# Load order, last output tile and stage shifts of a transformer block on one core

**Chip, cores, metric.** One Trainium2 chip (trn2), one of its cores. The metric is device time in microseconds (us) of one execution. A profile's span is 1.7 to 1.8 us shorter than the time of the same execution; where the text says "time" it means the former, where it says "span" the latter.

## The reference

Two sublayers over 2048 tokens of width 1024, in bfloat16, cut here to what matters:

```python
x = A_x                                            # (1, 2048, 1024)
h = x + A(layernorm(x), wq, wk, wv, wo, beta)      # 32 heads of 32, 4 segments of 512 tokens
#   per segment: p = softmax(causal q k^T), o = g * memory(q) + (1 - g) * (p v),  g = sigmoid(beta)
#   then the memory is updated with phi(k)^T v; after the 4th segment o @ wo
h2 = h + (silu(ln(h) @ w1) * (ln(h) @ w3)) @ w2    # inner width 3584
```

## The kernel before

The kernel writes no instruction order by hand. It builds a graph of operations, plans it with a list scheduler that has a cost for each operation, and then emits each engine's operations in the planned order. Each engine runs its queue strictly in that order. A table, `SHIFT`, moves each stage's priority a little; the table is the result of a search over plans. So any edit of the graph or of an assumed cost may reorder every engine.

Some words used below. A token tile is 128 tokens (`xs`). Its layer norm takes three steps: statistics, *apply* (subtract the mean, scale), and transposes on TensorE. PSUM is the memory that matmuls write to (`ps`); a result must be copied out before its bank is used again. A *score group* is the matmuls of q k^T for some heads; the *state matmuls* are those of phi(k)^T v that update the memory. A *dense* matmul here is one of 512 columns.

```python
SHIFT = {0: (113, 0), 1: (-194, 1), 2: (-667, 0), ...}     # stage: (rank shift, class shift)

    def dma(self, out, in_, cls=5, deps=(), eng="sp"):     # all loads and stores: one queue, SyncE
        ...
        o.bytes = n * SIZE[out.dtype]                      # the planner's landing time follows from this

    def constants(self):
        ...
        self.g.dma(self.beta[:, :], ..., cls=3)            # 8 KB, behind all the loads of class 0
        ...
        for n in range(4):                                 # "gcol": four small tanh on ScalarE
            self.act(self.gcol[r, :]..., bt, AF.Tanh, act_ns(8), cls=3, scale=0.5)

    def first_half(self):                                  # queries and keys of segment 0
        loads = [(self.xs[t][:, :], self.x2d[t * 128:(t + 1) * 128, :]) for t in range(4)]
        loads.insert(2, (wq[:, :, 0:256], sq[:, :, 0:256]))
        loads.insert(5, (wk[:, :, 0:256], sk[:, :, 0:256]))
        loads += [(wq[:, :, 256:512], ...), (wk[:, :, 256:512], ...), (wv[:, :, :], sv)]
        for out, in_ in loads:
            dma(out, in_, cls=0)
        for t in range(4):
            self.first_tile(t)         # statistics (VectorE for t = 0, 2; ScalarE for 1, 3), apply, transposes
        ...                            # then 16 projections by 128 columns of tokens

    def ffn_down(self, blk):
        ...
            cols = [(0, 512), (512, 256), (768, 256)] if t == 15 else [(0, 512), (512, 512)]
            for c0, n in cols:         # 28 matmuls, an add into ob, a store
```

The softmax here doesn't subtract the row's maximum and nothing guards it: scores larger than these inputs give would overflow.

## Time and profile before

| | before |
|---|---|
| time, first three runs | 896.26, 896.30, 896.68 us |
| span of the profiled run | 895.0 us |
| TensorE busy, as recorded (see the end of the experiments) | 880.6 us (98%) |
| TensorE idle in the first 20 us / after its last matmul | 4.0 us / 2.6 us |
| tile 1 ready on VectorE, applied | 7.76 us, 9.55 us |

Read it so: TensorE is the bound, so only what it waits for is worth anything. The largest single wait after the start is 1.23 us in the head. A late tile (2) blocks VectorE's queue, in which a ready tile (1) stands behind it. The lines themselves are in the prediction.

### The profile page before, as it was taken

What the parts mean: (1) busy time and instruction counts of PE and PEld (TensorE: products, weight loads), DVE (VectorE), ACT (ScalarE), POOL (GpSimd) and SP (SyncE); (2) the same over time, 40 slices, a digit from 0 to 9 for tenths busy, and PEclk for the clock granted to TensorE, in tenths of its full rate; (3) what the DMA queues carried; (4) which work ended last, traced back from release to release, by engine and by line L of the source; (5) the groups of instructions that cost most, each with busy time, mean ns of one, the idle gap of its engine ahead of it and who ended that gap; (6) DMA issues with size and microseconds to landing.
All of it is one profiled execution on the core that took longest, in us unless ns stands there. A gap on an engine that the chain in (4) does not pass through costs nothing.

```text
span 895.0 us, 13604 instructions
## 1 busy us (share of the span) xinstructions
PE 880.6 (98%) x5833; PEld 403.4 (45%) x5921; DVE 417.6 (47%) x631; ACT 287.9 (32%) x306; POOL 173.8 (19%) x226
## 2 busy tenths in 40 slices
PE   8999999999999999999999999999999999999998
PEld 5343444444444444444444444444444444444445
DVE  5784848585848485754555311211334333331111
ACT  6767766656565646111111100000111111110000
POOL 2553445353534343100200000000000000000000
PEclk9999999999999999999999999999999999999999
DMA  7899755634541221753475211113223221301110
GB/s 235 227 212 271 187 142 147 187 92 130 165 99 57 72 70 58 225 153 92 120 224 140 85 36 36 30 46 90 64 60 94 71 71 48 95 24 41 40 37 30
DMA packets 146540, 96.32 MB, mean 108 GB/s; under 512 B 45488, under 2 KB 133680, under 8 KB 146480
## 3 DMA queue, kind: packets, MB, share of 16 engines
q1 hardware_dynamic: 146480, 95.45, 38.8%
q8 instruction: 47, 0.77, 0.4%
q14 instruction: 13, 0.11, 0.0%
HBM read 76.55 MB, written 8.39 MB: 95 GB/s over the span
## 4 chain that ended last, share of the span: by engine, by line
PE 97%; issue 1%; DVE 1%; DMA 1%; ACT 0%; SPq 0%; ACTq 0%; DVEq 0%
PE ps L708 89%; PE ps L1107 4%; PE ps L1057 3%; DMA xs<-in_A_x_dram 1%; PE ps L985 0%; PE ps L1184 0%; ACT et L1069 0%; PE ps L1100 0%; DVE t L1260 0%; DVE hm L1265 0%; PE ps L720 0%; SPq L299 0%; DVE R L1163 0%; ACT sg L1257 0%; DVE Nsb L1171 0%
## 5 line engine op out<-in xcount | busy, mean ns | idle before, releaser
L708 PE MATMUL ps<-hnT,w1b 128*128 128x512 bf16 x876 | 218.4, 379 | 1.4 <-issue 0.3
L708 PE MATMUL ps<-hnT,w3b 128*128 128x512 bf16 x873 | 217.4, 379 | 1.5 <-issue 0.5
L1257 ACT ACTIVATE sg<-ps 128x512 bf16<-128x512 f32 x112 | 66.9, 597 | 403.1 <-PE ps L708 403.1
L708 PE MATMUL ps<-w2b,hm 128*128 128x512 bf16 (+1 forms) x907 | 195.3, 372 | 0.9
L1069 ACT ACTIVATE et<-ps 128x2048 bf16<-128x2048 f32 x80 | 150.0, 1875 | 39.3 <-PE ps L1057 38.9
L1260 DVE SCALAR_TENSOR_TENSOR t<-sg,ps 128x512 bf16<-128x512 bf16 x112 | 76.8, 685 | 169.4 <-ACT sg L1257 169.2
L708 PEld LDWEIGHTS ps<-w2b,hm 128*128 128x128 bf16 x924 | 90.4, 98 | 103.2
L708 PEld LDWEIGHTS ps<-hnT,w1b 128*128 128x128 bf16 x896 | 86.5, 98 | 105.5 <-issue 8.2
L708 PEld LDWEIGHTS ps<-hnT,w3b 128*128 128x128 bf16 x896 | 86.5, 98 | 105.4 <-issue 2.9
L1078 POOL TENSOR_SCALAR_AFFINE_SELECT et<-et 128x512 bf16<-128x512 bf16 x96 | 84.0, 881 | 126.2 <-ACT et L1069 126.0
L1265 DVE SCALAR_TENSOR_TENSOR hm<-t,ps 128x512 bf16<-128x512 bf16 x112 | 76.7, 686 | 50.5 <-PE ps L708 47.9
L1289 DVE TENSOR_TENSOR ob<-hr,ps 128x512 bf16<-128x512 bf16 (+1 forms) x33 | 22.1, 671 | 143.0 <-PE ps L708 143.0
L708 PE MATMUL ps<-wo,oT 128*128 128x512 bf16 x249 | 60.7, 380 | 0.6 <-issue 0.3
L708 PE MATMUL ps<-xnT,wp 128*128 128x512 bf16 (+1 forms) x345 | 59.7, 320 | 1.4 <-issue 0.6
L708 PE MATMUL ps<-hnT,wp 128*128 128x512 bf16 x250 | 59.0, 380 | 0.7 <-issue 0.6
L708 PEld LDWEIGHTS ps<-xnT,wp 128*128 128x128 bf16 x352 | 27.7, 98 | 26.9 <-issue 3.6
L708 PEld LDWEIGHTS ps<-wo,oT 128*128 128x128 bf16 x256 | 23.9, 98 | 29.8 <-issue 2.9
L708 PEld LDWEIGHTS ps<-hnT,wp 128*128 128x128 bf16 x256 | 23.6, 98 | 29.8 <-issue 3.8
L1200 POOL TENSOR_TENSOR oT<-Nsb,R 128x512 bf16<-128x512 f32 x23 | 35.8, 1569 | 4.1 <-DVE R L1197 4.1
L1163 DVE STREAM_TRANSPOSE R<-Rc 128x1024 f32<-128x1024 f32 x28 | 33.6, 1222 | 0.1
L1229 DVE TENSOR_TENSOR h<-h,ps 128x512 bf16<-128x512 bf16 x32 | 21.7, 680 | 25.1 <-PE ps L708 24.9
L1057 PE MATMUL ps<-qT,kT 32*128 32x128 bf16 (+3 forms) x512 | 31.7, 301 | 0.0
(82 smaller groups left out, 520.9 us busy)
## 6 DMA issues: line engine op xcount, KB each, us to landing
w1b<-in_B_w_dram SPq DMA_DIRECT2D x28, 512.0 KB, 3.9
w3b<-in_B_w_dram SPq DMA_DIRECT2D x28, 512.0 KB, 3.8
wp<-in_A_wv_dram SPq DMA_DIRECT2D x8, 1024.0 KB, 5.5
wp<-in_A_wq_dram SPq DMA_DIRECT2D x7, 1024.0 KB, 5.9
wp<-in_A_wk_dram SPq DMA_DIRECT2D x7, 1024.0 KB, 5.7
w2b<-in_B_w_dram SPq DMA_DIRECT2D x7, 1024.0 KB, 8.0
xs<-in_A_x_dram SPq DMA_DIRECT2D x16, 256.0 KB, 5.6
h<-in_A_x_dram SPq DMA_DIRECT2D x16, 256.0 KB, 3.7
```

The source lines that it names most:

```text
L708: return [e.matmul(p[0](gr), p[1], p[2], start=p[3], stop=p[4]) for p in part]
L1057: ins.append(e.matmul(self.bank(gr, j, 512 - 128 * kc, off), k[r, g0 + g, 128 * kc:128 * kc + 128], q[r, g0 + g, 128 * kc:512], start=True ...
L1069: return [e.activation(et[:, :, :], src, AF.Exp, scale=self.scale)]
L1078: self.pool_op(lambda e, v=v, pat=pat: e.affine_select(v, v, pattern=pat, compare_op=ALU.is_ge, fill=0.0, base=0, channel_multiplier=-1), ...
L1107: ins.append(e.matmul(self.ps[32 * i:32 * i + 32, b * 512 + 128 * kc:(b + 1) * 512], lhsT(i, kc, j), at[i, kc][:, j, :], start=kc == 0 and ...
L1163: return self.dve_op(lambda e: e.transpose(out, src), dve_ns(1024), [Rc[:, t, 2 * n:2 * n + 2, :]], [dst], 2)
L1200: self.either(lambda e, out=out, Ns=Ns, R1=R1: e.tensor_tensor(out, Ns, R1, op=ALU.add), 512, 2, [Ns, R1], [out], 2)
L1229: self.g.op("dve", dve_ns(512), lambda e, gr, hs=hs: [e.tensor_tensor(hs, hs, self.bank(gr), op=ALU.add)], reads=[hs], writes=[hs], cls=1, ...
L1257: self.g.op("act", act_ns(512), lambda e, gr, sg=sg: [e.activation(sg, self.bank(gr), AF.Tanh, scale=0.5)], writes=[sg], cls=0, group=gg)
L1260: e.scalar_tensor_tensor(t1, sg, 1.0, self.bank(gr), op0=ALU.add, op1=ALU.mult)], reads=[sg], writes=[t1], cls=0,
L1265: e.scalar_tensor_tensor(dst, t1, 0.5, self.bank(gr), op0=ALU.mult, op1=ALU.mult)], reads=[t1], writes=[dst], cls=0,
L1289: self.g.op("dve", dve_ns(n), lambda e, gr, hs=hs, ob=ob, n=n: [e.tensor_tensor(ob, hs, self.bank(gr, 0, n), op=ALU.add)], reads=[hs], wri ...
```

## The change

Its intent: load the third token tile before the first query weights, so that nothing blocks VectorE's queue; end the kernel on a smaller piece, so that less follows the last matmul; tell the planner how long the first loads really take, and search the table again for the new graph.

```diff
 SHIFT = {
-    0: (113, 0), 1: (-194, 1), 2: (-667, 0), ...
+    0: (-45, 0), 1: (-470, 0), 2: (43, 0), ...            # nearly every entry; cut here
-    def dma(self, out, in_, cls=5, deps=(), eng="sp"):
+    def dma(self, out, in_, cls=5, deps=(), scale=1.0):
-        o.bytes = n * SIZE[out.dtype]
+        o.bytes = n * SIZE[out.dtype] * scale
-        loads = [(self.xs[t][:, :], self.x2d[t * 128:(t + 1) * 128, :]) for t in range(4)]
-        loads.insert(2, (wq[:, :, 0:256], sq[:, :, 0:256]))
-        loads.insert(5, (wk[:, :, 0:256], sk[:, :, 0:256]))
-        loads += [...]
-        for out, in_ in loads:
-            dma(out, in_, cls=0)
+        x = [(self.xs[t][:, :], self.x2d[t * 128:(t + 1) * 128, :]) for t in range(4)]
+        loads = [x[0] + (1.04,), x[1] + (0.7,), x[2] + (1.2,),
+                 (wq[:, :, 0:256], sq[:, :, 0:256], 1.54), x[3] + (0.65,),
+                 (wk[:, :, 0:256], sk[:, :, 0:256], 0.74), ...]
+        for out, in_, scale in loads:
+            dma(out, in_, cls=0, scale=scale)
-            cols = [(0, 512), (512, 256), (768, 256)] if t == 15 else [(0, 512), (512, 512)]
+            cols = [(0, 512), (512, 256), (768, 128), (896, 128)] if t == 15 else [(0, 512), (512, 512)]
```

## The prediction

> **What bounds the kernel now.** I read the page first, then a table of stages, then the order of time at the two ends, then the list of waits. From the page, the busy line and the chain that ended last:
>
> ```profile
> PE 880.6 (98%) x5833; PEld 403.4 (45%) x5921; DVE 417.6 (47%) x631; ACT 287.9 (32%) x306; POOL 173.8 (19%) x226
> ...
> PE 97%; issue 1%; DVE 1%; DMA 1%; ACT 0%; SPq 0%; ACTq 0%; DVEq 0%
> ```
>
> TensorE is busy 98% of the span and makes up 97% of the chain; no other engine reaches half. So an edit counts only where it shortens TensorE's own stream or one of its few idle spells. The idle time is 895.0 - 880.6 = 14.4 us. The table of stages says where it lies (columns: window, its length, then busy time of PE, PEld, DVE, ACT, POOL, the granted clock, the DMA share and GB/s):
>
> ```profile
> 0.00:20.00 20.00, 16.00 (x181) 11.38 (x183) 9.70 (x28) 11.76 (x24) 5.06 (x22) 1.00 0.86 261
> ...
> 736.00:895.00 159.00, 155.62 (x738) 73.38 (x751) 38.21 (x57) 11.35 (x19) 0.00 (x0) 1.00 0.16 47
> ```
>
> The first 20 us hold 4.0 us of it, and the last stretch 3.4 us, of which 895.0 - 892.4 = 2.6 us follow the last matmul. The other 7 us are crumbs over 700 us. The granted clock is 1.00 everywhere, so no clock effect is to be had. The head, in order of time (start, length, engine, line, operation, tiles; in brackets the idle time before it and what ended it):
>
> ```profile
> 7.19 0.57 POOL L858 TENSOR_TENSOR rstd<-lnve,mhalf 128x1 f32<-128x1 f32 x1
> 7.70 0.90 PEld L708 LDWEIGHTS ps<-xnT,wp 128*128 128x128 bf16 x16 [0.74 <-DMA wp<-in_A_wq_dram]
> 7.70 1.07 PE L708 MATMUL ps<-xnT,wp 128*128 128x128 bf16 x16 [0.41 <-DMA wp<-in_A_wq_dram]
> 8.34 1.29 DVE L831 BATCH_NORM_STATS2 lnst<-xs 128x6 f32<-128x512 bf16 x2 [1.05 <-DMA xs<-in_A_x_dram]
> ...
> 9.55 0.72 DVE L862 TENSOR_SCALAR xs<-xs,lnst,rstd 128x512 bf16<-128x512 bf16 x2
> 10.00 0.55 PEld L720 LDWEIGHTS ps<-ident,xs 128*128 128x128 bf16 x8 [1.40 <-DVE xs L862]
> 10.00 0.72 PE L720 MATMUL ps<-ident,xs 128*128 128x128 bf16 x8 [1.23 <-DVE xs L862]
> ```
>
> This is the place the change aims at. Token tile 1's scale (rstd) is ready at 7.19 + 0.57 = 7.76 us, but VectorE applies it only at 9.55, because its in-order queue has the statistics of tile 2 ahead of it, and tile 2 lands at 8.34. TensorE, which has done its 16 matmuls for tile 0, sits idle 1.23 us until the apply. One load that comes late blocks a ready tile behind it. The tail:
>
> ```profile
> 887.20 0.69 DVE L1289 TENSOR_TENSOR ob<-hr,ps 128x512 bf16<-128x512 bf16 x1 [2.78 <-PE ps L708]
> 891.13 0.42 DVE L1289 TENSOR_TENSOR ob<-hr,ps 128x256 bf16<-128x256 bf16 x1 [3.24 <-PE ps L708]
> 892.44 0.42 DVE L1289 TENSOR_TENSOR ob<-hr,ps 128x256 bf16<-128x256 bf16 x1 [0.89 <-PE ps L708]
> ```
>
> After the last matmul: one 256-column add of 0.42 us, an issue, and a store whose landing took 1.6 us in this view of the queues. Last, who TensorE waited for (total us, times, longest):
>
> ```profile
> PE ps L708 <- issue: 3.0, 19, 0.2
> PE ps L720 <- DVE xs L862: 2.1, 2, 1.2
> PE ps L708 <- DVE oT L773: 1.2, 1, 1.2
> PE ps L985 <- issue: 1.1, 1, 1.1
> ```
>
> Beside the head there are 19 small gaps of about 0.16 us where the matmul form changes, and one 1.1 us spell inside a group of small state matmuls at 269.7 us, with nothing that the profile shows to wait for.
>
> **What the Trainium skill says.** "TensorE: Matmul & The Clock Gate", section "Wait — 56ns, not 53.3ns?", gives start to start N / 2.4 GHz plus about 2.5 ns: 55.6 ns for 128 columns, 215.7 ns for 512. The trace agrees: the chain has 52 matmuls of 128 columns in 2.90 us, 55.8 ns each. "DMA: Bandwidth & Descriptors", section "Specifications", says that line rate needs runs of at least 512 B and that shorter ones cost a read-modify-write; the new last stores have rows of 128 x 2 = 256 B. No run so far shows such rows: before, 1024 B rows landed in 1.7 us and 512 B rows in 1.6. The same page, "Queues, rings and completion order", says that descriptors on each engine are consumed in ring order. The trace agrees as to the loads: x0 releases its first user at 3.49 us, x1 at 4.14, the query weights at 7.70, x2 at 8.34, x3 at 9.06, the order of issue. Finally "Runtime: NRT & Kernel Launch", section "Instruction fetch mechanics", says that instructions are streamed in blocks of 16 KiB by the sequencer's own DMA; a late block would look like the spell at 269.7 us, but the trace doesn't prove it.
>
> **The change, part by part.** *Load order.* No byte is added. The 256 KB of x2 move ahead of the 512 KB of query weights. x2 follows x1 (4.14) by about what x1 followed x0, 0.65 us, or twice that where the weights' packets share the engines: estimate 4.8 to 5.4 us in place of 8.34. The weights land later by the time of x2's bytes, 8.34 - 7.70 = 0.64 us: 7.70 -> 8.3. x3 has the same bytes ahead of it as before and stays at 9.05, and so do all later loads. Now VectorE: tile 0's two applies end at 5.89 + 0.73 = 6.62; x2's statistics (1.29) end by about 7.9, and tile 1's apply runs at 7.8 to 8.6 in place of 9.55. Its transposes are done about when the weights arrive, and the wait of 1.23 us goes. But the weights cost 0.6 of it. Between 7.70 and the end of the first 128-column stage at 18.01 lie 10.31 us: idle 1.23 + 0.20, so work 8.88 (128 matmuls and 24 transposes at 55.8 ns are 8.5). From 8.3 without any idle time it ends at 17.2, 0.8 us sooner. Does x3 hold it up? In the kernel before x3 took from 9.06 (ScalarE's first pass) to 14.50 (transposes). Until then TensorE has 96 matmuls and 16 transposes, 6.5 us with their switches, which from 8.3 reach 14.8. So x3 is just in time, and a bubble of 0.2 to 0.3 around its copy out of PSUM is likely. Net: **-0.6 us**, and since TensorE is the chain from there on, it reaches the end.
>
> *Last tile in pieces of 128.* TensorE: 28 matmuls of 256 columns at 256 / 2.4 + 2.5 = 109.2 ns become 56 at 55.8: +0.07 us, weight loads hidden as in the first stage, where the same shape ran at that rate. The last add: 0.69 for 512 and 0.42 for 256 columns put 128 at about 0.285: -0.135 us. The store: 64 KB fewer took 0.1 us off before, so 32 KB may take 0.05, and rows of 256 B may take that back: 0. Net: **-0.1 us**. It rests on the last two pieces ending apart; before, they ended 892.44 - 891.13 = 1.31 us apart.
>
> *Table of shifts and load scales.* They change no instruction's work, only the order in which the kernel's own planner puts them. Every engine's order will differ. What it can win is the crumbs: 19 form changes of 0.16 us, the spell of 1.1 us, and form changes that the trace counts as busy. What it can't win: the second block of the feed-forward part runs 50 matmuls in 10.79 us, 215.8 ns each, the rate above. The old table was tuned as well; a rebuilt one was presumably kept because it did better, and the load times that the planner now assumes look fitted, so I lean to **-0.5 us**, with a spread of about 1 us either way.
>
> Sum: -0.6 - 0.1 - 0.5 = -1.2 us on the median of 896.3: **895.1 us**, 0.13% less.
>
> **The rivals.** (1) The new order turns one wait into another: TensorE starts at 8.3 in place of 7.7 and then waits for x3 or the key weights. For it: the DMA engines are 0.86 busy in the first 20 us and no byte goes away. Against: the key weights' first matmuls ran by about 11 us before, and TensorE now has work until then. The head would give 0, the sum -0.6: 895.7 us. (2) The table carries the change: fewer splits of the attention stages and no spell at 269.7. For it: nearly every entry is new, and 18 to 438 us holds the mixed stage. Against: TensorE idles little there, and each score group must interrupt the dense stream. It would give -2 to -2.5: 893.5 us. (3) The table, made on a plan and not on the chip, opens a new wait of 1 us, or instruction fetch falls badly: +0.5, 896.8 us. (4) The tail gains nothing, as the last two pieces end together and queue on VectorE, or 256 B rows land late: +0.1 to +0.3 on the sum.
>
> **Range and chances.** Spread of the head 0.3, of the tail 0.15, of the table 1.0, together about 1.1 us: for 8 in 10, 893.6 to 896.4. The repeats of one kernel span 0.4 us, well inside. 2% of 896.3 is 17.9 us, more than all of TensorE's idle time, so faster by over 2% can't come from this: 0.005. Slower by that needs a plan gone badly wrong: 0.005. Within 2%: 0.99.
>
> **What would show it.** Right: x2's statistics start near 6.3 to 6.6 us with no DMA wait before them, tile 1's apply by 8.6, query matmuls near 8.3 with the DMA of the weights as releaser, no idle spell of 1.2 us before the transposes, and the last 128-column projection matmul at 17.2 to 17.6. A last add of about 0.28 us, and 2.4 us from last matmul to end in place of 2.6. Wrong: the first-stage end still near 18.0, an idle TensorE before x3's transposes of over 0.6 us, a store of 256 B rows that lands later than 1.8 us, or a change of TensorE's idle plus form changes between 20 and 440 us larger than 1.5 us.

## More of the kernel before

`beta` has 32 numbers. It is used late: the gate g is first needed when the first segment's output is put together, over 50 us into the kernel.

## The result, and the profile after

| | before | changed |
|---|---|---|
| time, median (range), same set of runs | 896.49 us (896.26 to 898.08, 4 runs) | 896.30 us (896.10 to 897.36, 4 runs) |
| ratio, 95% interval | | 0.9996 (0.9979 to 1.0014) |
| span of the profiled run | 895.0 us | 895.6 us |

Ratios here and below are the mean time of one kernel's fast runs over that of the other's in the same rounds, so not quite the ratio of the medians. The three runs of the changed kernel without a profile had spans of 894.3 to 894.6 us, so the profiled one is a bad one of its kind; its traces still show what went wrong, and the repeat (e1) below says how much of it is typical.

1.2 us were forecast, 0.2 us came. The page of the changed kernel, its busy line and the chain that ended last:

```profile
PE 881.3 (98%) x5861; PEld 403.6 (45%) x5949; DVE 424.6 (47%) x639; ACT 284.6 (32%) x299; POOL 173.8 (19%) x226
...
PE 95%; DMA 2%; issue 1%; SPq 1%; DVE 1%; ACT 0%; ACTq 0%
PE ps L698 87%; PE ps L1098 4%; PE ps L1048 3%; SPq L289 1%; DMA beta<-in_A_beta_dram 1%; DMA wp<-in_A_wq_dram 1%; PE ps L976 0%; PE ps L1175 0%; DVE R L1154 0%; ACT et L1060 0%; PE ps L1091 0%; DVE t L1251 0%; DVE hm L1256 0%; ACT sg L1248
```

TensorE's work is the same as before (a matmul line is L698 here and L708 before, the edit moved the lines). The chain, which before began with a token tile (`xs`), now runs through something new: `beta`, the 8 KB gate load. In order of time:

```profile
6.33 1.28 DVE L821 BATCH_NORM_STATS2 lnst<-xs 128x6 f32<-128x512 bf16 x2
...
7.71 0.84 PE L698 MATMUL ps<-xnT,wp 128*128 128x128 bf16 x12 [0.63 <-DMA wp<-in_A_wq_dram]
7.86 0.73 DVE L852 TENSOR_SCALAR xs<-xs,lnst,rstd 128x512 bf16<-128x512 bf16 x2
...
8.39 0.65 PE L710 MATMUL ps<-ident,xs 128*128 128x128 bf16 x8
...
9.91 2.01 SPq L289 DMA_DIRECT2D beta<-in_A_beta_dram  x1
...
18.53 0.90 ACT L673 ACTIVATE gcol<-beta 32x8 f32<-32x8 bf16 x4 [2.57 <-DMA beta<-in_A_beta_dram]
...
19.45 1.08 ACT L721 ACTIVATE qT<-ps 128x512 bf16<-128x512 f32 x2
...
20.10 1.90 PE L698 MATMUL ps<-xnT,wp 128*128 128x512 bf16 x8 [1.49 <-ACT qT L721]
```

The upper half is the gain as it was planned: tile 2's statistics run at 6.33 us with no wait, tile 1 is applied at 7.86 in place of 9.55, its transposes start at 8.39 in place of 10.00, and nothing idles before them. The lower half is the loss. The gate load is issued at 9.91 us behind 1 MB of value weights and lands at 18.5. The new order puts the four gate activations on ScalarE ahead of the copies of two query projections out of PSUM (`qT<-ps`). ScalarE stands 2.57 us, the copies come late, and TensorE, whose next projection goes into a PSUM bank that such a copy empties, stands 1.49 us. In the kernel before, the same load landed about as late (issued 10.59, 7.5 us to landing), but ScalarE came to the gates at 19.20 and did not wait:

```profile
10.59 1.93 SPq L299 DMA_DIRECT2D beta<-in_A_beta_dram  x1
...
19.20 0.88 ACT L683 ACTIVATE gcol<-beta 32x8 f32<-32x8 bf16 x4
```

The list of TensorE's waits in the changed kernel says it in total (us, times, longest):

```profile
PE ps L698 <- issue: 3.7, 22, 0.3
PE ps L698 <- ACT qT L721: 1.5, 1, 1.5
PE ps L698 <- DVE oT L763: 1.2, 1, 1.2
...
PE ps L710 <- DVE xs L852: 0.4, 1, 0.4
```

The wait for the gate's followers (1.5) is new; the wait for tiles to be applied is down from 2.1 us to 0.4. The tail, last adds of the output:

```profile
891.11 0.42 DVE L1280 TENSOR_TENSOR ob<-hr,ps 128x256 bf16<-128x256 bf16 x1 [2.39 <-PE ps L698]
892.23 0.29 DVE L1280 TENSOR_TENSOR ob<-hr,ps 128x128 bf16<-128x128 bf16 x1 [0.70 <-PE ps L698]
893.35 0.29 DVE L1280 TENSOR_TENSOR ob<-hr,ps 128x128 bf16<-128x128 bf16 x1 [0.83 <-PE ps L698]
```

The last add takes 0.29 us, and 895.6 - 893.3 = 2.3 us follow the last matmul, where 2.6 did.

**Theory.** The head won what the order of loads promised, and the new order gave it back by putting the gate activations, and with them ScalarE's queue, behind a load that lands at 18 us. **Rivals.** (R1) The head's gain is lost to another limit anyway (third tile, key weights, score groups), and the gate load only shows the slack. (R2) The wandering of the landing times is larger than what the order moves. (R3) The table is what counts, for better or worse.

### The profile page after: what moved, and what is told of

It reads as the page before. It is cut to its first block, busy times and chain, and to the rows that moved or that the text cites. A ratio compares the mean times of both kernels' runs of the same rounds, so it can differ in the third digit from the quotient of the medians.

```text
span 895.6 us, 13656 instructions
## 1 busy us (share of the span) xinstructions
PE 881.3 (98%) x5861; PEld 403.6 (45%) x5949; DVE 424.6 (47%) x639; ACT 284.6 (32%) x299; POOL 173.8 (19%) x226
## 3 DMA queue, kind: packets, MB, share of 16 engines
HBM read 76.55 MB, written 8.39 MB: 95 GB/s over the span
## 4 chain that ended last, share of the span: by engine, by line
PE 95%; DMA 2%; issue 1%; SPq 1%; DVE 1%; ACT 0%; ACTq 0%
PE ps L698 87%; PE ps L1098 4%; PE ps L1048 3%; SPq L289 1%; DMA beta<-in_A_beta_dram 1%; DMA wp<-in_A_wq_dram 1%; PE ps L976 0%; PE ps L1175 0%; DVE R L1154 0%; ACT et L1060 0%; PE ps L1091 0%; DVE t L1251 0%; DVE hm L1256 0%; ACT sg L1248 0%; ACT gcol L673 0%
## 5 line engine op out<-in xcount | busy, mean ns | idle before, releaser
L698 PE MATMUL ps<-hnT,w1b 128*128 128x512 bf16 x870 | 217.5, 379 | 1.6 <-DVE R L1154 0.2
L698 PE MATMUL ps<-hnT,w3b 128*128 128x512 bf16 x880 | 217.8, 379 | 1.3 <-issue 0.6
L698 PE MATMUL ps<-w2b,hm 128*128 128x512 bf16 (+2 forms) x935 | 195.4, 366 | 0.9
L698 PEld LDWEIGHTS ps<-w2b,hm 128*128 128x128 bf16 x952 | 90.9, 98 | 102.9
L698 PEld LDWEIGHTS ps<-hnT,w1b 128*128 128x128 bf16 x896 | 86.8, 98 | 105.7 <-issue 7.4
L698 PEld LDWEIGHTS ps<-hnT,w3b 128*128 128x128 bf16 x896 | 86.4, 98 | 105.2 <-issue 2.9
L1280 DVE TENSOR_TENSOR ob<-hr,ps 128x512 bf16<-128x512 bf16 (+2 forms) x34 | 22.3, 655 | 142.9 <-PE ps L698 142.9
L698 PE MATMUL ps<-xnT,wp 128*128 128x512 bf16 (+1 forms) x347 | 60.4, 320 | 3.1 <-ACT qT L721 1.5
L698 PE MATMUL ps<-wo,oT 128*128 128x512 bf16 x251 | 61.5, 380 | 0.6 <-issue 0.5
L698 PE MATMUL ps<-hnT,wp 128*128 128x512 bf16 x249 | 59.1, 380 | 1.1 <-issue 1.0
L698 PEld LDWEIGHTS ps<-xnT,wp 128*128 128x128 bf16 x352 | 28.0, 98 | 29.5 <-issue 2.8
L698 PEld LDWEIGHTS ps<-wo,oT 128*128 128x128 bf16 x256 | 23.8, 98 | 29.9 <-issue 3.3
L698 PEld LDWEIGHTS ps<-hnT,wp 128*128 128x128 bf16 x256 | 23.6, 98 | 30.2 <-issue 4.4
L1048 PE MATMUL ps<-qT,kT 32*128 32x128 bf16 (+3 forms) x512 | 31.7, 301 | 0.0
L698 PE MATMUL ps<-wp,xnT 128*128 128x512 bf16 x121 | 30.1, 380 | 0.8 <-issue 0.6
## 6 DMA issues: line engine op xcount, KB each, us to landing
w2b<-in_B_w_dram SPq DMA_DIRECT2D x7, 1024.0 KB, 10.2
```

The source lines that it names most:

```text
L698: return [e.matmul(p[0](gr), p[1], p[2], start=p[3], stop=p[4]) for p in part]
L1048: ins.append(e.matmul(self.bank(gr, j, 512 - 128 * kc, off), k[r, g0 + g, 128 * kc:128 * kc + 128], q[r, g0 + g, 128 * kc:512], start=True ...
L1280: self.g.op("dve", dve_ns(n), lambda e, gr, hs=hs, ob=ob, n=n: [e.tensor_tensor(ob, hs, self.bank(gr, 0, n), op=ALU.add)], reads=[hs], wri ...
```

## The experiments

Most experiments don't plan again: they take a kernel's finished plan and move single operations in an engine's order, so nothing else changes. The helper, called after the planner:

```diff
+    def move(self, starts):                       # {operation number: new place in time}
+        for i, start in starts.items():
+            self.g.ops[i].start = start
+        for row in self.g.order.values():         # each engine's order, sorted again
+            row.sort(key=lambda o: (o.start, o.pos))
+            ...
```

Operation 13 is the gate load, 14 to 17 are the gate activations, 18 and 19 two small VectorE operations on their result, 22 and 23 the third and fourth load of the list. All kernels below gave the correct result. The kernel before ran beside each set, and its own times wander: 896.2 to 898.56 us (median 897.1) in the first set (e1 to e4), 896.15 to 898.24 (median 897.67) in the third (e9 to e12); the second set (e5 to e8) shares the runs of the first and one more. So the kernels of one set are best compared with each other.

### e1: the changed kernel again

No edit.

> The changed kernel once more, as the yardstick of this set. Both theories: 896.3 us give or take 0.3, ratio to the kernel before 0.999 to 1.001; in the profile ScalarE again waits 2 to 3 us for the small gate load (beta) and TensorE about 1.5 us behind it, near 18.6 to 20.1 us.

Measured: 895.90 us (895.43 to 896.30, 5 runs), ratio to before 0.9987 (0.9975 to 0.9999). The time is 0.4 us under the expected 896.3, just outside the 0.3 allowed for, and the profile fits only in part:

```profile
8.88 0.84 PE L698 MATMUL ps<-xnT,wp 128*128 128x128 bf16 x12 [1.49 <-DMA wp<-in_A_wq_dram]
...
21.43 0.39 PE L1048 MATMUL ps<-qT,kT 32*128 32x512 bf16 x4
```

ScalarE waited for the gate load, but 0.9 us only, and TensorE not at all behind it. It had begun 1.2 us later, since the query weights landed at 8.88 us in place of 7.71. The first score group (L1048) starts at 21.43 us here and at 21.93 in the first profile. So the two waits do not add up: when the weights come late, TensorE reaches the place where it would stand later, and the gate load has landed by then. The gate load acts as a floor under this stretch, whatever the start. In this profile the floor cost TensorE nothing: from the first query matmul to the first score group it took 12.55 us, as with the early load (e2: 12.57). How often the 1.5 us are lost in runs without a profile is not shown; only their times speak, and those are 0.6 to 1.2 us above the kernels below that take the wait away (e2, e3, e9, e11).

### e2: the gate load issued early

```diff
+        self.move({13: 355.0})        # changed kernel: beta ahead of the second half of wq
```

> The changed kernel with one thing moved: the 8 KB gate load is issued before the second half of the query weights instead of after the value weights. Theory (the new head won about 1.2 us and the late gate load, with ScalarE's in-order queue behind it, gave it back): no wait for beta, TensorE's idle spell of 1.5 us near 18.6 us goes, the time falls by 1.0 to 1.5 us to about 895.0, ratio to before 0.9983 to 0.9989. Rival (the head's gain is lost to another limit anyway, x3, key weights or the score groups that follow): the spell moves to another releaser and the time stays within 0.4 us of 896.3.

Measured: 894.66 us (894.45 to 894.90, 5 runs), 1.24 us less than e1 on the same chip, ratio to before 0.9973 (0.9961 to 0.9985). The load was issued at 3.76 us and took 6.4 us, so it landed at 10.2 in place of 18. TensorE in the head:

```profile
7.55 0.83 PE L698 MATMUL ps<-xnT,wp 128*128 128x128 bf16 x12 [0.49 <-ACT xnT L721]
8.50 0.72 PE L710 MATMUL ps<-ident,xs 128*128 128x128 bf16 x8
...
13.67 6.52 PE L698 MATMUL ps<-xnT,wp 128*128 128x128 bf16 x67
20.12 0.39 PE L1048 MATMUL ps<-qT,kT 32*128 32x512 bf16 x4
```

There is no gap in it from 8.50 on, and the first score group starts at 20.12 us. The time fell by what the theory said, which speaks against R1. But the query matmuls also began 1.33 us sooner than in e1, and that is the whole difference of the two profiles at the first score group (20.12 against 21.43), so this pair does not show the gates' part. That the edit itself brings the weights sooner is not seen: the first query matmul comes at 7.71, 8.88, 8.45 and 7.87 us with the late gate load (changed, e1, e3, e10) and at 7.55, 8.01, 8.51 and 8.54 with the early one (e2, e6, e9, e11). And e3, which moves no load, gains as well.

### e3: the gate activations late, the load as it was

```diff
+        self.move({14: 23720.0, 15: 23721.0, 16: 23722.0, 17: 23723.0, 18: 25971.0, 19: 25971.5})
```

> The changed kernel with the load where it was, but the four small gate activations put some 7 us later in ScalarE's order, and the two VectorE operations on them likewise. Theory: the same gain as with the early load, 1.0 to 1.5 us (about 895.0), since nothing waits for the load then. Rival (it is the traffic of the load and not the order of ScalarE that costs): no gain here, within 0.4 us of 896.3.

Measured: 895.18 us (894.83 to 898.04, 6 runs; five of them 894.83 to 895.62), ratio 0.9985 (0.9973 to 0.9997), 0.7 us less than e1 by the medians. By the ratios, which the run at 898.04 pulls up, it is only 0.2 us, so this rests on five runs of six. The gain is there without touching the load, if less than forecast. In the profile TensorE began its query matmuls at 8.45 us, ran without a gap and reached the first score group at 20.91. The load landed at 17.8 us, as late as ever, and nobody waited. This speaks for the place in ScalarE's queue as what costs, and against the traffic; e10 gives the dose.

### e4: the kernel before, only the two loads swapped

```diff
+        self.move({22: 180.0, 23: 120.0})     # kernel before: third tile ahead of the query weights
```

> The kernel before with its old table and its old order on all compute engines, only the issue of the third token tile and of the first query weights swapped. Theory: tile 1's apply comes about 1 us sooner, TensorE's idle spell before the transposes falls from 1.23 to about 0.2, the time falls by 0.7 to 1.1 us to about 895.4, as the gate activations stand behind the keys there. Rival (the weights come 0.6 us later and eat it): 0 to 0.4 us.

Measured: 896.67 us (895.74 to 897.56, 5 runs), ratio 0.9998 (0.9985 to 1.0011). A miss by the time, and the profile shows why. The head did what was forecast: the transposes of tile 1 start at 9.09 us in place of 10.00, the first score group at 20.06 in place of 20.76. At the state matmuls near 268 us the 0.70 us are still there, and are lost inside that group. The kernel before:

```profile
269.22 0.51 PE L985 MATMUL ps<-v,pkn 128*32 128x33 bf16 x42
...
270.81 0.32 PE L985 MATMUL ps<-v,pkn 128*32 128x33 bf16 x22 [1.07 <-issue]
```

and with the swap:

```profile
268.52 0.51 PE L985 MATMUL ps<-v,pkn 128*32 128x33 bf16 x42
...
270.63 0.32 PE L985 MATMUL ps<-v,pkn 128*32 128x33 bf16 x22 [1.59 <-issue]
```

TensorE stops after the 42nd of 64 small matmuls and goes on at 270.6 to 270.8 us, whether it came at 269.2 or at 268.5. It arrived 0.70 us sooner and left 0.18 us sooner. The releaser is given as "issue": the list of waits names nothing that it waited for (more on this under "What stays open").

### e5: the kernel before, only the last piece split

```diff
-            cols = [(0, 512), (512, 256), (768, 256)] if t == 15 else ...
+            cols = [(0, 512), (512, 256), (768, 128), (896, 128)] if t == 15 else ...
```

> The kernel before with the last output piece of 256 columns cut into two of 128, old table, old loads; the order differs in the last 60 or so matmuls alone. Theory (prediction's tail): matmuls 0.07 us longer, last add 0.29 in place of 0.42 us, last matmul to end of span 2.3 us in place of 2.6; together about -0.2 us, so the landmarks in the profile show it and the time, within 0.3 us of before, does not. Rival (rows of 256 B make the last store land late): last matmul to end stays at 2.6 us or grows.

Measured: 897.0 us (896.80 to 897.88, 4 runs), ratio 0.9999 (0.9984 to 1.0013). The tail is as in the theory: last add 0.29 us, and 896.1 - 893.82 = 2.3 us after the last matmul. The time shows nothing, as forecast. This run showed something else:

```profile
34.55 2.76 PE L708 MATMUL ps<-xnT,wp 128*128 128x512 bf16 x11 [1.26 <-DMA wp<-in_A_wk_dram]
```

The key weights of the second half, issued at 26.13 us, released TensorE at 34.55 only. The first profile of the same order had no such wait (issued at 26.09). So under the old order a wait of over 1 us comes and goes with that load's landing.

### e6: the early gate load, the last piece not split

```diff
         self.move({13: 355.0})
-            cols = [(0, 512), (512, 256), (768, 128), (896, 128)] if t == 15 else ...
+            cols = [(0, 512), (512, 256), (768, 256)] if t == 15 else ...
```

> The kernel with the early gate load, but the last tile in two pieces of 256 as before. Theory: 0.2 to 0.3 us slower than with the split, 894.9 us; last matmul to end back at 2.6 us. Rival (the split is worth nothing or costs): 894.7 us or less.

Measured: 895.18 us (894.62 to 895.75, 4 runs), ratio 0.9979 (0.9967 to 0.9992). By the times, within their scatter of 1.1 us, this can't be told from e2 (another set). The two profiles can be laid over each other, since they are level late in the kernel (the same ScalarE activation starts at 732.59 us in both). From there to the last matmul the split costs 0.08 us (890.62 against 890.54), and from the last matmul to the end of the span it saves 0.28 us (2.28 against 2.56). Net 0.2 us, of which the shorter add is 0.13.

### e7: all of the change but the new order

```diff
+        self.move({22: 180.0, 23: 120.0})     # kernel before, with the split of e5
```

> The kernel before with old table, the issue of the third tile and the first query weights swapped, and the last piece split: all of the change but the new order on the compute engines. If the new table is worth something by itself, this stays at 896.3 to 896.6 us, 1.5 us or more behind the new table with the early gate load, with the spell inside the state matmuls near 270 us (1.1 and 1.6 us so far under the old table) as the difference. Rival (table worth nothing): within 0.5 us of 894.7.

Measured: 896.59 us (896.02 to 897.45, 4 runs), ratio 0.9996 (0.9981 to 1.0010): the first branch. The state matmuls stopped for 0.58 us, less than forecast, and the key weights of the second half were waited for again, 1.01 us at 33.83. So the old order can't keep the head's gain.

### e8: new order, early gate load, old order of loads

```diff
+        self.move({13: 355.0, 22: 180.0, 23: 120.0})     # changed kernel: query weights first again
```

> The new table and the early gate load, but the first query weights issued ahead of the third tile again, as before. Theory (the load order is worth what the idle spell was): VectorE waits for tile 2 until about 8.3 us, tile 1's transposes slip to about 10 us, TensorE idles over 1.2 us in the head, the time rises by 0.8 to 1.4 us from 894.7 to about 895.8. Rival (the landing times wander by more than the swap moves, the order hardly counts): within 0.4 us of 894.7.

Measured: 895.86 us (895.32 to 896.15, 4 runs), ratio 0.9986 (0.9973 to 0.9999). Against e2 that is 1.2 us more by time (sets differ) and 1.4 us by span (894.3 against 892.9). The profile has the old wait in the old place:

```profile
7.42 0.83 PE L698 MATMUL ps<-xnT,wp 128*128 128x128 bf16 x12 [0.31 <-ACT xnT L721]
9.47 0.72 PE L710 MATMUL ps<-ident,xs 128*128 128x128 bf16 x8 [1.22 <-DVE xs L852]
```

Against e9, the same kernel as e2 run once more, it is 0.6 us by time. So the old order of loads brings the idle spell back, and costs 0.6 to 1.2 us; R2 is too strong, though not empty: see e9.

### e9: the early gate load once more

No edit against e2.

> The changed kernel with the early gate load once more, to see whether it holds: 894.5 to 895.2 us, ratio to before 0.9965 to 0.9985, no wait for beta in the profile, no idle spell of TensorE over 0.6 us after its query matmuls begin. If the first result was luck of the loads' landing: 895.7 us or more.

Measured: 895.27 us (894.88 to 895.63 in four runs, 897.50 in one), ratio 0.9981 (0.9968 to 0.9994). It holds, though 0.1 us over the top of the expected range and 0.6 us slower than in e2. The profile's query weights landed at 8.51 us, and the first score group came at 20.98 in place of 20.12: the landing of one 512 KB load is what most of that is. The five profiles with the new table and the early gate load (e2, e6, e8, e9, e11; e8 with the old order of loads) have first query matmuls at 7.55, 8.01, 7.42, 8.51 and 8.54 us. In the first three a copy of ScalarE (`xnT`) released them and the weights were there before; in the last two the weights did.

### e10: the gate load later still

```diff
+        self.move({13: 14485.0})      # changed kernel: behind four token tiles of the next segment
```

> The changed kernel with the 8 KB gate load issued still later, behind the four token tiles of the next segment. Dose test. Theory: the load lands near 20.5 to 21.5 us in place of 18.0 to 18.5, ScalarE waits for it that much longer, TensorE's spell behind it grows by 2 to 3 us, time 898 to 899 us. Rival (the wait is hidden or belongs to something else): within 0.5 us of the changed kernel's 896.3.

Measured: 900.39 us (899.23 to 901.28, 4 runs), ratio 1.0030 (1.0015 to 1.0046). The load was issued at 14.64 us:

```profile
21.04 0.90 ACT L673 ACTIVATE gcol<-beta 32x8 f32<-32x8 bf16 x4 [4.91 <-DMA beta<-in_A_beta_dram]
...
22.61 3.23 PE L698 MATMUL ps<-xnT,wp 128*128 128x512 bf16 x8 [3.82 <-ACT qT L721]
```

ScalarE waited 4.91 us in place of 2.57, TensorE 3.82 in place of 1.49: the 2.3 us of the theory. But the time rose by more than that and than the 898 to 899 us expected: 4.1 us over the changed kernel's 896.3. The 8 matmuls after the wait took 3.23 us; after the short wait they took 1.90. The table of stages names it (the number after POOL's is the granted clock):

```profile
18.00:22.00 4.00, 0.79 (x7) 0.38 (x5) 0.72 (x2) 0.86 (x5) 0.00 (x0) 0.99 0.21 73
22.00:26.00 4.00, 3.38 (x12) 1.15 (x12) 4.00 (x9) 2.59 (x4) 0.00 (x0) 0.58 0.00 0
```

After 3.8 us without work TensorE was granted 0.58 of its clock over the next 4 us. "TensorE: Matmul & The Clock Gate" in the Trainium skill, section "What's actually happening", puts the fall to half rate after an idle window of about 3.4 us; this run agrees, and in the changed kernel, after 1.49 us, the clock stayed at 1.00.

### e11: early load and late activations

```diff
+        self.move({13: 355.0, 14: 23720.0, 15: 23721.0, 16: 23722.0, 17: 23723.0, 18: 25971.0, 19: 25971.5})
```

> Both cures at once, early gate load and late gate activations. If the gate load is the one thing, the two don't add: within 0.4 us of the early load alone, 894.5 to 895.0. If moving the activations off the queue before the first scores helps by itself: 894.2 or less.

Measured: 895.01 us (894.50 to 895.37, 4 runs), ratio 0.9973 (0.9960 to 0.9987), against 895.27 for the early load in the same set. Within the noise the two cures don't add, so they cure one thing.

### e12: the new table with the old loads

The kernel before, with the new `SHIFT` and nothing else; it is planned anew.

> The kernel before with the new table of shifts and nothing else: load order, assumed load times and last tile as before. The table's entries only fit the plan that they were made for: slower by 8 us or more, by small idle spells of TensorE between 20 and 440 us. Rival (the table is a better order whatever the loads): within 2 us of 896.5.

Measured: 912.62 us (one run, so of unknown state; granted clock 0.996). TensorE's waits in this profile, the largest first:

```profile
PE ps L1047 <- ACT et L1059: 6.2, 6, 2.2
PE ps L698 <- DVE t L1250: 3.1, 5, 1.0
PE ps L1097 <- issue: 2.3, 1, 2.3
```

A table belongs to the graph and the assumed times that it was searched for. The converse, the old table with all the rest of the change, has no run: it stops in the planner with 1285 operations left. It is a single run, but 15 us slower, so R3 in its plain form ("a better order as such") falls.

### The landmarks side by side

From the profiles, in us. First score group means the first matmul of the scores (12 dense matmuls of 512 columns precede it under the old order and 16 under the new, 4 x 0.216 = 0.86 us more work, so the two halves of the table are not compared in that column). Spell means TensorE's stop inside the state matmuls near 270 us; a dash is none listed.

| run | first query matmul | first score group | spell | last matmul ends | span |
|---|---|---|---|---|---|
| before (old order) | 7.70 | 20.76 | 1.07 | 892.42 | 895.0 |
| e4 loads swapped | 8.13 | 20.06 | 1.59 | 892.25 | 894.9 |
| e5 split | 7.73 | 20.80 | 1.03 | 893.82 | 896.1 |
| e7 swapped, split | 8.15 | 20.33 | 0.58 | 892.65 | 895.0 |
| changed (new order) | 7.71 | 21.93 | 0.56 | 893.32 | 895.6 |
| e1 changed again | 8.88 | 21.43 | - | 892.09 | 894.4 |
| e2 gate load early | 7.55 | 20.12 | - | 890.62 | 892.9 |
| e3 gates late | 8.45 | 20.91 | - | 890.97 | 893.3 |
| e9 gate load early | 8.51 | 20.98 | 0.19 | 891.56 | 893.9 |
| e10 gate load later | 7.87 | 25.77 | 0.36 | 896.98 | 899.3 |

Under the new order without a wait for the gate, first query matmul to first score group is about 12.5 us (e2 12.57, e3 12.46, e9 12.47), so the start decides. In the changed kernel it is 14.22: the wait of 1.49 and a little more. Best of all versions is the changed kernel with the gate load issued early (e2 and e9) or with both moves (e11): 894.45 to 895.63 us in thirteen of fourteen runs, 0.2 to 0.3% less than the kernel before by ratio. That is under both kernels, with intervals that leave out 1, though far under the 2%.

### What the small gaps were

Neither the prediction nor the experiments asked what the 19 gaps of 0.16 us are. The trace lacks matmul records there. A matmul comes with one weight load, yet the profile before counts 5833 matmuls and 5921 weight loads; the profiles of the changed kernel, e1 and e2 count 5861 and 5949. The profiles of e9, e10 and e11 have all 5949 of both, and such gaps are gone (e9 lists one wait of TensorE on "issue" at its dense matmuls, e2 lists 22). At one place, first e2, then e9:

```profile
33.64 0.81 PE L698 MATMUL ps<-wp,xnT 128*128 128x512 bf16 x3 [0.16 <-issue]
```

```profile
34.27 1.04 PE L698 MATMUL ps<-wp,xnT 128*128 128x512 bf16 x4
```

With all records TensorE is busy 888.5 of 893.9 us (e9) and 887.8 of 893.6 (e11). So the real idle time was about 7 us in the kernel before (an estimate: 14.4 less the 7 or so by which the busy time rises between e2 and e9), nearly all of it at the two ends and in the one spell near 270 us.

## Why the prediction was right or wrong

The range (893.6 to 896.4 us) held the 896.3 us, and "within 2%" was right. That is partly luck: the value lies 0.1 us inside the edge of a range that was 2.8 us wide because of the table's spread, and the gain was given back in a way the prediction did not reckon. The point, 895.1, was not right: of 1.2 us forecast, 0.2 came at first. The repeat (e1) gave 895.90 with a ratio of 0.9987. So the change alone is worth 0.04 to 0.13% by the two ratios, and the first of them can't be told from nothing.

- **What bounds it: right, the idle time misread.** TensorE's recorded busy time is 880.6 and 881.3 us (88 matmul records missing in both), and each gain and loss found above is an idle spell of TensorE. No other engine became the bound. But of the 14.4 us of idle time about half, the "crumbs", was missing records and could not be won.
- **Load order, mechanism: right.** The statistics of tile 2 at 6.33 us (6.3 to 6.6 forecast), tile 1's apply over by 8.6, no spell before the transposes. e8 confirms it backwards: with the old order of loads the spell of 1.22 us is back, and 0.6 (against e9) to 1.2 us (against e2) of time with it.
- **Load order, the weights: sized wrong, and from one sample.** The forecast moved the weights' landing from 7.70 to 8.3 us by the bytes put ahead of them. Where these weights release the first query matmul under the new order of loads and table (changed, e1, e9, e10, e11), they do so at 7.71 to 8.88 us, so this landing wanders by more than the 0.64 us that was reckoned. In the first profile it hadn't moved at all (7.71), x3, said to stay at 9.05, released its first user at 8.41, and the head won more than forecast. The end of the first stage can only be reckoned back, since dense matmuls are mixed into it. In the kernel before, 18.01 us is the first score group's start less 12 dense matmuls of 0.216 and 0.16 us. The same sum in the changed kernel, with 16 dense matmuls and without the wait of 1.49, gives 21.93 - 3.45 - 1.49 - 0.16 = 16.8 us; 17.2 was forecast.
- **"Since TensorE is the chain from there on, it reaches the end": this is the step that failed.** A gain reaches the end only if the rest of the order lets TensorE run ahead. Under the new order ScalarE's queue had a load that lands at 18 us in front of two PSUM copies, so TensorE could not pass that point before 20.1 us in the first profile, however soon it started. Shown by e2, e9, e3 and e11 (take the wait away in two ways: 0.6 to 1.2 us less than e1 by the medians, not additive; e9 and e11 are of another set) and by e10 (more of it: more time, and the wait in the trace). The first rival in the prediction, one wait turned into another, was the right kind; it named the third tile and the key weights, and neither was it.
- **Table, -0.5 +- 1: not borne out as one number.** Of what it was to win, the 19 form changes were not there. The new order did two things at once. It is better in the middle: the spell in the state matmuls is 0 to 0.56 us in its profiles, 0.58 to 1.59 under the old one, and no profile of it waits over 0.5 us for weights of the second half, where e5 and e7 wait 1.26 and 1.01. And it is worse at one place, the gates. With that place mended the full change is 1.7 to 2.4 us faster than before by the ratios (0.9981 and 0.9973 of 897 us); all but the new order (e7) gives 0.4 us (0.9996).
- **Tail, -0.1: right in kind, -0.2 by one pair of profiles (e2, e6).** Matmuls +0.08 (forecast +0.07), add -0.13 (-0.135), and the rest, the store, -0.15 where 0 was forecast, by fear of 256 B rows: the stores of 64 KB took 1.6 us to land and those of 32 KB 1.5. The two last pieces end 1.1 us apart, so they don't queue.

**What stays open.** Why TensorE stops inside the state matmuls is not shown by any experiment, but the traces point at its instructions. Within one order the stop always falls at the same place, after the 42nd of the 64 matmuls in the four profiles of the old order and after the 25th in the three of the new order that have it (changed, e9, e10), whatever the time. "Runtime: NRT & Kernel Launch", section "Instruction fetch mechanics", describes instructions being fetched in blocks of 16 KiB. The traces hold 47 such packets on queue q8. At the page's 256 instructions a block they are about 12,000 instructions (an estimate), and only TensorE has so many: 12,094 records in e9, every other engine under 800. Leave out e12, which has another order again. In all seven profiles with a stop, TensorE went on 1.9 to 2.3 us after one of these packets started. In the six without, the packet started 2.0 to 2.3 us before the group did. The later it came, the longer the stop: it started 1.65 us before the group in e9 (stop 0.19), 1.27 in the changed kernel (0.56), 0.37 in the kernel before (1.07) and 0.03 in e4 (1.59). So a late block of instructions is the likely cause; no run moved such a packet, and what makes it late is open. Nor is it shown why the first loads' landing wanders, or how much of the scatter of the kernel before (896.05 to 898.56 us) is the wait for second-half key weights seen in e5 and e7.

## What to carry to other kernels

Before crediting a saved wait to the end, walk every in-order queue past the place where the saving is made, and ask of each item whether something that lands at a fixed time stands in it; a tiny load at the end of a long load list is such a floor for everything queued behind its first user. Issue small loads early or put their users late; either one is enough. A searched order is fitted to the landing times assumed for it, so look at one trace of the new order for the waits that the search could not see. And before small gaps are counted as time to win, compare the number of matmuls with that of weight loads in the profile: what is missing there looks idle.

## What the Trainium skill lacked or had wrong

- "DMA: Bandwidth & Descriptors", section "Specifications", says that runs below 512 B are off line rate. For a single last store it did not matter: 32 KB in rows of 256 B landed in 1.5 us, 64 KB in rows of 512 B in 1.6, 128 KB in rows of 1024 B in 1.7.
- The same page, section "Anatomy of one DMA — SWDGE (gpsimd) path", gives about 2 us of fixed cost, for loads issued from GpSimd; there is no figure in it for a small load issued behind megabytes of others. Here 8 KB took 6.3 to 8.6 us from the start of its issue to landing, and the issue itself took 1.8 to 2.9 us in the first 13 us of the kernel, against 0.42 us at 14.64 us (e10). The landing of the first query weights wandered from 7.71 to 8.88 us under one order of loads.
- "Runtime: NRT & Kernel Launch", section "Instruction fetch mechanics", calls the cost of crossing a block boundary mostly hidden. Here a stop of 0.19 to 1.59 us inside a group of 64 small matmuls ended 1.9 to 2.3 us after an instruction packet started, in seven of thirteen profiles: likely a block that came late, though not shown by experiment.
- No page that I read warns that a profile can lack matmul records and so show idle time that isn't there: 88 of 5949 here, in gaps of mostly 0.16 us.
